# Attention's softmax denominators inverted on one row per head and spread by DMA, and 13 more exponential pairs on VectorE

## The chip, the cores and the metric

One Trainium2 chip, one core. The metric is the device time of one execution in microseconds (us), lower is better. Each kernel is timed as the median of several runs. In the profile PE is TensorE, PEld its weight loads, DVE is VectorE, ACT is ScalarE, POOL is GpSimd and SP is SyncE, whose queue issues nearly all DMAs.

## The reference

The input is x, 2048 tokens by 1024, bfloat16. Four residual layers run one after the other: A, B, A, B, with the same weights in both rounds.

```
x = x + A(layernorm(x)); x = x + B(layernorm(x)); x = x + A(layernorm(x)); x = x + B(layernorm(x))

A:  32 heads of 32; phi(q) = concat(softmax(q w_phi), softmax(-q w_phi)), the same for k
    o = phi(q) (phi(k)^T v) / (phi(q) sum(phi(k)) + 1e-6);  return o @ wo
B:  32 heads of 32; scores = q k^T * 32**-0.5
    o = softmax(scores) v;  return o @ wo
```

A is linear attention and B is plain, non-causal softmax attention over all 2048 keys. The change is in B.

## The kernel before

Nothing is issued in the order in which the source reads. Every piece of work is registered as an `Op` with an engine, an estimated duration, dependencies, the buffers that it needs and a due time (`prio`). `Sched.run` (L145) is a list scheduler: it plays the operations on modelled engines, takes the earliest due one whose buffers can be had, and so fixes one order per engine, which is the order of the program. SBUF is one arena out of which buffers are taken by class; `QUOTA` (L257) says how many of a class may live at once. PSUM's eight banks are given out in the same way: two groups of three banks for scores (class S), bank 6 for the accumulator (class acc), bank 7 for everything that fills in between (`FIL`). Where PE would idle too long, the scheduler puts filler matmuls in (L1248, L1253).

`attention` (L971) is called once per round, after layer A and the first keys, values and queries. It runs over 32 turns; a turn is one chunk of 512 queries (qc, four of them) with one group of four heads (g, eight of them). `turns` (L1100) lists them: first chunks 0 and 1 for every group, then chunks 2 and 3. `pos` is a turn's number, 0 to 31. Every turn has two halves (pp), each with two heads' outputs: 16 key blocks, written as d (8) and pairs, with four units per step of d. A unit is 128 keys by 512 queries of one head.

Three units are one group: three score matmuls (L1006) into three banks, one ACTIVATE with Exp over 1536 columns (L1012, ACT), then per unit two matmuls into the accumulator (L1042): one with v, one with a matrix of ones, so that the 128 partitions of bank 6 hold the numerators of two heads in 64 rows and their denominators, each repeated on 32 rows, in the other 64. At the end of each half DVE copies the bank into a buffer of class T (L1057), which frees it for the next half.

Some units do not go to ACT. `exp_dve` (L931) takes two units of head 3 of the group and computes the exponential by a polynomial on DVE: a score matmul into bank 7 (L944), two DVE steps that read it (L949, L952), twice, then two steps on exponents (L955, L958), three on the polynomial (L963) and the product (L966). `EXTRA` (L270) lists, for each round and turn, which pairs (pp, d) go that way; `LEAD` makes them due half a turn early.

At the end of a turn the denominators are inverted (L1083 to L1095). In the halves of one turn they lie on opposite partitions, so two DMAs of 64 rows each bring them from the two T buffers into one buffer (class den) of 128 partitions by 512; four DVE reciprocals of 128 columns (L1087) invert it, and two DVE products (L1091) write the turn's 128 by 512 bfloat16 output tile (class oT). The last turn of a round (`end`) has a way of its own, without DMA (L1064 to L1082).

Meanwhile the other work of the layer fills in: keys and values of later groups (L839 on DVE, copies L831 into kT), queries (L847, L863, L852 and L853; chunks 2 and 3 are stored to DRAM by L865 and come back by L871 to L873), weights (L522), the output projection (L899, or L928 at the end), and in the first round also the next layer A's norms and keys.

Of the kernel before, what the change touches and what calls it, by code (L numbers as in the profile page):

```python
# [11 lines left out]
ALU = mybir.AluOpType  # L12
AX = mybir.AxisListType
BF16 = mybir.dt.bfloat16
F32 = mybir.dt.float32
# [5 lines left out]
C512 = 512  # L21
# [26 lines left out]
class Sched:  # L48
# [11 lines left out]
    def op(self, eng, dur, fn, deps=(), bufs=(), prio=0.0, lat=None, mode=None):  # L60
        o = Op(eng, dur, LAT[eng] if lat is None else lat, fn, tuple(bufs), prio, mode, len(self.ops))
        for d in deps:
            if d is not None:
                d.out.append(o)
                o.ndep += 1
        for b in o.bufs:
            b.left += 1
        self.ops.append(o)
        return o
# [75 lines left out]
    def run(self):  # L145
# [25 lines left out]
        while left:  # L171
# [85 lines left out]
QUOTA = {"pk": 3, "pv": 2, "kv": 1, "ln": 2, "mm": 2, "cmp": 2, "bc": 4, "num": 1, "wt": 4, "fil": 2,  # L257
         "e": 6, "vp": 6, "e1": 4, "vp1": 4, "E": 5, "q2": 3, "kt": 3, "w2": 8, "w2o": 3, "oT": 26, "T": 4, "den": 2,
         "lnt": 6, "lnw": 2, "lnw1": 1, "eq": 8, "ns": 4, "cw": 6, "hl": 6, "oc": 2, "slab": 7, "slabk": 3, "fin": 4,
         "rs": 8, "pkf": 1, "part": 8, "w2r": 1,  # L260
         "xs": 1, "xu": 2, "xg": 2, "xx": 2, "E1": 3}
SPELL = 3.4
KEEP = 0.75
# [3 lines left out]
POW2_0 = 0.998010015430466  # L267
POW2_C = (-2.753493604392706, 3.611980637904819, -2.738565741928622)
LEAD = 5.0
EXTRA = (lambda i: [(i % 2, 2)] if 12 <= i < 17 else [],  # L270
         lambda i: [(0, 2), (1, 2)] if 16 < i < 30 and i % 4 else [(i % 2, 2)] if 8 <= i < 30 else [])


def act_us(n):
# [3 lines left out]
def dve_us(n):  # L278
    return n / 960 + 0.15
# [6 lines left out]
def kernel(  # L286
# [11 lines left out]
    nc = tc.nc  # L298
    P = nc.NUM_PARTITIONS
    _, S, D = A_x.shape  # L300
    PO = D // P
    G = PO
    NC = S // C512
# [14 lines left out]
    dram_p = ctx.enter_context(tc.tile_pool(name="scratch", bufs=1, space=bass.MemoryType.DRAM))  # L318
# [23 lines left out]
    for j in range(4):  # L342
# [4 lines left out]
        out=rep[:].rearrange("p (x j) -> p x j", j=4),  # L347
        in_=J_bf[:].rearrange("p (j d) -> p d j", d=32)[:, 0:8, :],
    )
    nc.vector.tensor_copy(out=fold[:], in_=ident[:, 0:32])  # L350
    for a in range(1, 4):
        nc.vector.tensor_tensor(
            out=fold[:], in0=fold[:], in1=ident[:, 32 * a:32 * a + 32], op=ALU.add
# [4 lines left out]
        out=selb[:].rearrange("p (j d) -> p j d", d=32),  # L358
        in_=pick[:].unsqueeze(2).to_broadcast([P, 4, 32]),
# [10 lines left out]
    wdq_v = wd_q[:].rearrange("(po pi) f -> pi po f", pi=P)  # L370
    wdk_v = wd_k[:].rearrange("(po pi) f -> pi po f", pi=P)

    qd = dram_p.tile([P, 2 * G * C512], BF16, tag="qd")
    qd_v = qd[:].rearrange("p (c g n) -> p c g n", c=2, g=G)
    xd = dram_p.tile([P, 3 * PO * C512], BF16, tag="xd")
# [3 lines left out]
    op = sch.op  # L379

    def sb(cls, *dims, dt=BF16):
        n = 1
        for d in dims:
            n *= d
        b = Buf("sb", -(-n * (4 if dt == F32 else 2) // 64) * 64, cls)
        b.with_ = ()

        def v():
            ap = arena[:, b.at // 2:b.at // 2 + n * (2 if dt == F32 else 1)]
            if dt == F32:  # L390
                ap = ap.bitcast(F32)
            if len(dims) == 2:
                ap = ap.rearrange("p (a b) -> p a b", a=dims[0])
            elif len(dims) == 3:
                ap = ap.rearrange("p (a b c) -> p a b c", a=dims[0], b=dims[1])
            return ap

        return b, v
# [16 lines left out]
    def dma(prio, fn, deps=(), bufs=(), q="SP", kb=256, issue=0.55):  # L415
        return op(q, issue, fn, deps, bufs, prio, lat=2.0 + kb / 200.0)
# [450 lines left out]
    def q_back(g, c, prio, away):  # L867
        q_b, q_v = sb("q2", 2, C512)
        src = qd_v[:, c - 2, g, :]
        return q_b, q_v, [  # L870
            dma(prio, lambda: nc.sync.dma_start(out=q_v()[:, 0, :], in_=src), [away], [q_b], kb=128),  # L871
            dma(prio, lambda: nc.sync.dma_start(out=q_v()[64:128, 1, :], in_=src[0:64]), [away], [q_b], kb=64),
            dma(prio, lambda: nc.sync.dma_start(out=q_v()[0:64, 1, :], in_=src[64:128]), [away], [q_b], kb=64)]  # L873
# [97 lines left out]
    def attention(base, kT, vT, q_of, gate, extra):  # L971
# [14 lines left out]
        n = 0  # L986
        i = 0
        while i < len(units):
# [5 lines left out]
            qc, g, pp, d, j = grp[0]  # L994
            prio = base + 10 * pos[(qc, g)] + 5 * pp + 0.5 * d
# [7 lines left out]
            def sfn(grp=grp, s_v=s_v):  # L1003
# [9 lines left out]
                out=e_v()[:, 0:w * C512], in_=s_v(), func=ACT.Exp, scale=4 * math.log(2)),  # L1013
# [7 lines left out]
        if True:  # L1021
            for qc, g in turns:
                T = []
                end = (qc, g) == turns[-1]
                for pp in range(2):
                    a_b, a_v = ps("acc", [(6,)])
                    last = None
                    for d in range(8):
                        prio = base + 10 * pos[(qc, g)] + 5 * pp + 0.5 * d
# [30 lines left out]
                prio = base + 10 * pos[(qc, g)] + 12  # L1060
                lo_, hi_ = slice(0, 64), slice(64, 128)
                d_b, d_v = sb("den", C512, dt=F32)
                r_b, r_v = d_b, d_v
                if end:  # L1064

                    o_b, o_v = sb("oT", C512)
                    rc = [op("DVE", 128 * 8 / 960 + 0.12, lambda b=b, T=T, r_v=r_v: nc.vector.reciprocal(
                        out=r_v()[hi_, b * P:(b + 1) * P], in_=T[0][1]()[hi_, b * P:(b + 1) * P]),
                        [T[0][2]], [d_b, T[0][0]], prio) for b in range(4)]
                    s = [op("DVE", dve_us(512), lambda o_v=o_v, r_v=r_v, T=T: nc.vector.tensor_tensor(  # L1070
                        out=o_v()[lo_, :], in0=T[0][1]()[lo_, :], in1=r_v()[hi_, :], op=ALU.mult),
                        rc, [o_b, d_b, T[0][0]], prio)]
                    l_b, l_v = sb("den", C512, dt=F32)
                    ln = op("ACT", act_us(512), lambda l_v=l_v, a_v=a_v: nc.scalar.activation(
                        out=l_v()[lo_, :], in_=a_v()[lo_, :], func=ACT.Ln), [last], [a_b, l_b], prio)
                    ln = op("ACT", act_us(512), lambda l_v=l_v: nc.scalar.activation(
                        out=l_v()[lo_, :], in_=l_v()[lo_, :], func=ACT.Exp, scale=-1.0), [ln], [l_b], prio)
                    s.append(op("DVE", dve_us(512), lambda o_v=o_v, l_v=l_v, a_v=a_v: nc.vector.tensor_tensor(
                        out=o_v()[hi_, :], in0=a_v()[hi_, :], in1=l_v()[lo_, :], op=ALU.mult),
                        [ln], [o_b, l_b, a_b], prio))  # L1080
                    oTs[qc][g] = (o_b, o_v, s)
                    continue  # L1082
                m1 = dma(prio, lambda d_v=d_v, T=T: nc.sync.dma_start(out=d_v()[hi_, :], in_=T[0][1]()[hi_, :]),  # L1083
                         [T[0][2]], [d_b, T[0][0]], kb=128)
                m2 = dma(prio, lambda d_v=d_v, T=T: nc.sync.dma_start(out=d_v()[lo_, :], in_=T[1][1]()[lo_, :]),
                         [T[1][2]], [d_b, T[1][0]], kb=128)
                rc = [op("DVE", 128 * 8 / 960 + 0.12, lambda b=b, d_v=d_v, r_v=r_v: nc.vector.reciprocal(  # L1087
                    out=r_v()[:, b * P:(b + 1) * P], in_=d_v()[:, b * P:(b + 1) * P]), [m1, m2], [d_b], prio)
                    for b in range(4)]
                o_b, o_v = sb("oT", C512)  # L1090
                s = [op("DVE", dve_us(512), lambda a=a, b=b, k=k, o_v=o_v, r_v=r_v, T=T: nc.vector.tensor_tensor(  # L1091
                    out=o_v()[a, :], in0=T[k][1]()[a, :], in1=r_v()[b, :], op=ALU.mult),
                    rc, [o_b, r_b, T[k][0]], prio)
                    for k, (a, b) in enumerate(((lo_, hi_), (hi_, lo_)))]
                oTs[qc][g] = (o_b, o_v, s)  # L1095
        return oTs, so

# [9 lines left out]
        out=phi()[32 * j:32 * j + 32, :, 32 * j:32 * j + 32],  # L1107
        in_=A_w_phi.rearrange("(g j) i f -> j i g f", j=4)[j]), [phi_0], [phi_b], kb=16) for j in range(4)]
# [14 lines left out]
    for layer in range(2):  # L1123
# [21 lines left out]
        else:  # L1145
            wq_s = [slab("slab", second - 15 + fc, wdq_v[:, :, fc * C512:(fc + 1) * C512], C512, [store["q"][fc]])
                    for fc in range(2)]
            for c in range(NC - 1):
                x_b, x_v = sb("xn", PO, C512)
                xnA[c] = (x_b, x_v, [dma(second - 20 + 20 * c, lambda c=c, x_v=x_v: nc.sync.dma_start(  # L1150
                    out=x_v(), in_=xd_v[:, c, :, :]), [xnA[c]], [x_b], kb=1024)] * 4)
# [11 lines left out]
        for c in range(NC):  # L1163
            pr = second + 20 * c
            o_b, o_v = sb("oc", G, C512)
# [21 lines left out]
        for g in range(G):  # L1187
            pr = at + 10 * pos[(0, g)]
            w = slab("w2", pr - 11, B_w[:, :, g * P:(g + 1) * P], P) if g else wq0
            for qc in range(NC):  # L1190
# [3 lines left out]
                else:  # L1194
                    away = q_away(g, qc, pr + 2 + 6 * (qc - 2), w, FIL)
                    q_of[(qc, g)] = q_back(g, qc, at + 10 * pos[(qc, g)] - 12, away)
        oTs, last_s = attention(at, kT, vT, q_of, gate, EXTRA[layer])
        if last:
            bo_s = [slab("slab", at + 160 + fc, B_o[:, :, fc * C512:(fc + 1) * C512], C512) for fc in range(2)]
# [14 lines left out]
        qc = NC - 1  # L1214
# [9 lines left out]
        if not last:  # L1224
            r_b, r_v = sb("w2r", 2, D)
# [11 lines left out]
        if not last:  # L1237

            kv = new_kv()
            for c, p0 in ((0, 190), (1, 220), (2, 265)):  # L1240
# [4 lines left out]
                    out=xd_v[:, c, :, :], in_=xv()), fin, [xb], kb=1024)  # L1245
# [43 lines left out]
```

## Time and profile before

| | us |
|---|---|
| median of 3 runs | 2510.38 (2509.66 to 2510.57) |
| the profiled execution | 2511.27 |
| its span, first to last instruction | 2509.5 |
| attention of round one, first to last L1012 or L1057 | about 358 to 1346 |
| attention of round two | about 1566 to 2499 |
| granted TensorE clock, mean | 0.994 |

The profiled execution is 0.9 us above the median, and 1.8 us of it lie outside its span. A turn takes about 30 us. Busy shares are given per engine over the span and in 40 slices of it; the waits name the engine that came last.

### The profile page before, as it was taken

What the parts mean: (1) busy time and instruction counts of PE and PEld (TensorE: products, weight loads), DVE (VectorE), ACT (ScalarE), POOL (GpSimd) and SP (SyncE); (2) the same over time, 40 slices, a digit from 0 to 9 for tenths busy, and PEclk for the clock granted to TensorE, in tenths of its full rate; (3) what the DMA queues carried; (4) which work ended last, traced back from release to release, by engine and by line L of the source; (5) the groups of instructions that cost most, each with busy time, mean ns of one, the idle gap of its engine ahead of it and who ended that gap; (6) DMA issues with size and microseconds to landing.
All of it is one profiled execution on the core that took longest, in us unless ns stands there. A gap on an engine that the chain in (4) does not pass through costs nothing.

```text
span 2509.5 us, 62924 instructions
## 1 busy us (share of the span) xinstructions
PE 2368.6 (94%) x27872; PEld 893.4 (36%) x27872; DVE 1468.5 (59%) x2003; ACT 2145.4 (85%) x1897; POOL 26.1 (1%) x72
## 2 busy tenths in 40 slices
PE   7999999999999999999999999999999999999998
PEld 4443433333333333333333444333333333333333
DVE  6997653333356345654646766333356578687854
ACT  6335558999999999999996465699999999999998
POOL 0000000000000000000000000000000000000000
PEclk9999999999999999999999999999999999999999
DMA  9110012111121222222323001111121100110000
GB/s 219 33 44 1 22 21 48 35 36 44 41 62 42 56 54 69 77 66 69 114 65 116 1 5 38 36 36 35 40 62 27 35 27 27 29 33 27 25 25 27
DMA packets 185282, 117.39 MB, mean 47 GB/s; under 512 B 103344, under 2 KB 175024, under 8 KB 184240
## 3 DMA queue, kind: packets, MB, share of 16 engines
q1 hardware_dynamic: 183952, 111.26, 16.7%
q8 instruction: 218, 3.57, 0.6%
q10 hardware_dynamic: 1056, 2.10, 0.3%
q14 instruction: 56, 0.46, 0.1%
HBM read 62.46 MB, written 15.73 MB: 31 GB/s over the span
## 4 chain that ended last, share of the span: by engine, by line
ACT 46%; PE 31%; issue 12%; DVE 8%; SPq 1%; DMA 1%; ACTq 0%; DVEq 0%
ACT arena L1012 43%; PE psum L421 14%; PE psum L425 5%; PE psum L1042 5%; PE psum L1006 4%; DVE arena L616 1%; SPq L456 1%; PE psum L1253 1%; PE psum L780 1%; ACT arena L612 1%; DVE arena L625 1%; DVE arena L963 1%; DVE arena L662 1%; DVE arena L510 1%; DVE arena L514 1%
## 5 line engine op out<-in xcount | busy, mean ns | idle before, releaser
L1012 ACT ACTIVATE arena<-psum 128x1536 bf16<-128x1536 f32 x1342 | 1812.4, 1566 | 50.5 <-PE psum L1006 43.7
L1042 PE MATMUL psum<-arena 128*32 128x512 bf16 x4096 | 699.0, 385 | 11.6 <-ACT arena L1012 8.4
L1042 PE MATMUL psum<-arena,ones_bf 128*32 128x512 bf16 x4096 | 700.3, 386 | 0.0
L1006 PE MATMUL psum<-arena 32*128 32x512 bf16 x4022 | 522.8, 383 | 74.6 <-ACT arena L1012 68.3
L425 PE MATMUL psum<-arena 128*32 128x512 bf16 x8256 | 576.3, 380 | 4.9 <-DVE arena L625 1.3
L421 PE MATMUL psum<-arena 128*128 128x512 bf16 x2032 | 474.2, 383 | 18.1 <-DVE arena L514 5.4
L1006 PEld LDWEIGHTS <-arena 32*128 32x128 bf16 x4022 | 163.4, 91 | 574.8 <-issue 564.9
L421 PEld LDWEIGHTS <-arena 128*128 128x128 bf16 x2032 | 193.6, 98 | 265.8 <-issue 47.6
L425 PEld LDWEIGHTS <-arena 128*32 128x32 bf16 x8256 | 212.3, 96 | 209.8 <-issue 53.9
L1042 PEld LDWEIGHTS <-arena 128*32 128x32 bf16 x4096 | 165.8, 94 | 271.6 <-issue 246.5
L1087 DVE RECIPROCAL arena<-arena 128x128 f32<-128x128 f32 x248 | 212.9, 913 | 44.7 <-DMA arena<-arena 44.4
L1253 PE MATMUL psum<-xT,zero 128*32 128x512 bf16 x2712 | 218.5, 382 | 0.0
L839 DVE CAST arena<-psum 128x512 bf16<-128x512 f32 x112 | 77.3, 690 | 238.5 <-PE psum L425 238.1
L1042 PEld LDWEIGHTS <-ones_bf 128*32 128x32 bf16 x4096 | 158.4, 94 | 62.7 <-issue 50.8
L1057 DVE COPY arena<-psum 128x512 f32<-128x512 f32 x126 | 86.8, 689 | 157.3 <-PE psum L1042 155.6
L963 DVE SCALAR_TENSOR_TENSOR arena<-arena 128x1024 f32<-128x1024 f32 x111 | 135.6, 1222 | 2.3
L612 ACT ACTIVATE arena<-psum 128x512 bf16<-128x512 f32 x80 | 42.8, 600 | 86.1 <-PE psum L421 57.8
L742 ACT ACTIVATE arena<-psum 128x512 bf16<-128x512 f32 x128 | 69.8, 597 | 41.5 <-PE psum L421 32.0
L625 DVE TENSOR_TENSOR arena<-psum,arena 128x1024 bf16<-128x1024 f32 x64 | 78.3, 1224 | 39.6 <-PE psum L425 35.5
L510 DVE TENSOR_TENSOR arena<-xT,arena 128x1024 f32<-128x1024 bf16 x64 | 77.9, 1219 | 35.2 <-ACT arena L499 34.8
L1253 PEld LDWEIGHTS <-zero 128*32 128x32 bf16 x2712 | 70.3, 97 | 64.5 <-issue 16.8
L514 DVE TENSOR_TENSOR arena<-arena 128x1024 bf16<-128x1024 f32 x64 | 77.4, 1223 | 23.9 <-ACT arena L504 22.6
(100 smaller groups left out, 1428.3 us busy)
## 6 DMA issues: line engine op xcount, KB each, us to landing
arena<-arena SPq DMA_DIRECT2D x124, 128.0 KB, 2.2
arena<-in_A_wqkv_dram SPq DMA_DIRECT2D x10, 1024.0 KB, 5.5
arena<-in_B_wqkv_dram SPq DMA_DIRECT2D x32, 256.0 KB, 3.1
arena<-arena SPq DMA_DIRECT2D x256, 32.0 KB, 1.9
arena<-in_B_wo_dram SPq DMA_DIRECT2D x32, 256.0 KB, 3.0
arena<-wd_k SPq DMA_DIRECT2D x8, 1024.0 KB, 5.7
arena<-in_A_wo_dram SPq DMA_DIRECT2D x4, 1024.0 KB, 7.1
arena<-in_B_wqkv_dram SPq DMA_DIRECT2D x4, 1024.0 KB, 5.4
```

Of the source, the lines that this page charges most:

```text
L421: nc.tensor.matmul(out_, lhsT=lhsT, rhs=rhs, start=start, stop=stop, skip_group_check=True)
L425: nc.tensor.matmul(out_[ks, :], lhsT=lhsT[:, ks], rhs=rhs, start=start, stop=stop, tile_position=(0, 32 * k), skip_group_check=True)
L510: s1 = op("DVE", dve_us(1024), lambda pr=pr, w_v=w_v: nc.vector.tensor_tensor(out=w_v(), in0=xT[:, pr, csl(c)], in1=m_v().unsqueeze(1).to_ ...
L514: fin.append(op("DVE", dve_us(1024), lambda pr=pr, w_v=w_v: nc.vector.tensor_tensor(out=xv()[:, pr, :], in0=w_v(), in1=r_v().unsqueeze(1). ...
L625: ml = op("DVE", dve_us(1024), lambda vpv=vpv, wv_=wv_, sv=sv: nc.vector.tensor_tensor(out=wv_()[:, :, :, 0:DH], in0=vpv().rearrange("p (h ...
L963: last = [op("DVE", dve_us(1024), lambda i=i, c=c: nc.vector.scalar_tensor_tensor(out=x_v(), in0=(x_v() if i else g_v()), scalar=c, in1=g_ ...
L1006: nc.tensor.matmul(out=s_v()[:, x * C512:(x + 1) * C512], lhsT=kT[g][1]()[r, pp, d * P:(d + 1) * P], rhs=q_of[(qc, g)][1]()[r, (pp + j // ...
L1012: ex = op("ACT", act_us(w * C512), lambda s_v=s_v, e_v=e_v, w=w: nc.scalar.activation(out=e_v()[:, 0:w * C512], in_=s_v(), func=ACT.Exp, s ...
L1042: nc.tensor.matmul(out=a_v()[col:col + 32, :], lhsT=v_v()[:, kc % 4, o:o + DH] if what == 0 else ones_bf[:], rhs=ev()[:, x * C512:(x + 1) ...
L1057: cp = op("DVE", dve_us(512), lambda t_v=t_v, a_v=a_v: nc.vector.tensor_copy(out=t_v(), in_=a_v()), [last], [a_b, t_b], prio - 4)
L1087: rc = [op("DVE", 128 * 8 / 960 + 0.12, lambda b=b, d_v=d_v, r_v=r_v: nc.vector.reciprocal(out=r_v()[:, b * P:(b + 1) * P], in_=d_v()[:, b ...
L1253: nc.tensor.matmul(psum[32 * k:32 * k + 32, 6 * C512:7 * C512], lhsT=zero[:], rhs=xT[:, 0, 0:C512], start=False, stop=False, tile_position ...
```

## The change

The inversion of the denominators is done on one row per head instead of 32 equal ones, and `exp_dve` takes more units. The `end` turn is as it was.

- From each T buffer a DMA takes one row of each of the two heads (512 numbers) and lays it over 32 partitions by 16 columns; the two DMAs fill a buffer of 128 by 16 (class cden).
- One DVE reciprocal of 16 columns inverts all four heads' rows.
- A DMA writes the 128 by 16 numbers to a DRAM scratch `rd`, where they are four rows of 512; another reads each row back onto 32 partitions, into the den buffer.
- The two products read it on the same partitions as the numerators.
- `EXTRA` lists 10 pairs instead of 5 in the first round and 40 instead of 32 in the second.

```diff
-         "rs": 8, "pkf": 1, "part": 8, "w2r": 1,
+         "rs": 8, "pkf": 1, "cden": 2, "part": 8, "w2r": 1,
...
-EXTRA = (lambda i: [(i % 2, 2)] if 12 <= i < 17 else [],
-         lambda i: [(0, 2), (1, 2)] if 16 < i < 30 and i % 4 else [(i % 2, 2)] if 8 <= i < 30 else [])
+EXTRA = (lambda i: [(0, 2), (1, 2)] if 12 <= i < 17 else [],
+         lambda i: ([(0, 2), (1, 2)] if i % 3 else [(0, 2), (0, 5), (1, 4)]) if 16 <= i < 30 else [(i % 2, 2)] if 8 <= i < 16 else [])
...
+    rd = dram_p.tile([2 * NC * G * 4, C512], F32, tag="rd")
+    rd_v = rd[:].rearrange("(t h) n -> t h n", h=4)
+    gone = []
...
-                m1 = dma(prio, lambda d_v=d_v, T=T: nc.sync.dma_start(out=d_v()[hi_, :], in_=T[0][1]()[hi_, :]),
-                         [T[0][2]], [d_b, T[0][0]], kb=128)
-                m2 = dma(prio, lambda d_v=d_v, T=T: nc.sync.dma_start(out=d_v()[lo_, :], in_=T[1][1]()[lo_, :]),
-                         [T[1][2]], [d_b, T[1][0]], kb=128)
-                rc = [op("DVE", 128 * 8 / 960 + 0.12, lambda b=b, d_v=d_v, r_v=r_v: nc.vector.reciprocal(
-                    out=r_v()[:, b * P:(b + 1) * P], in_=d_v()[:, b * P:(b + 1) * P]), [m1, m2], [d_b], prio)
-                    for b in range(4)]
+                c_b, c_v = sb("cden", 16, dt=F32)
+                at_d = rd_v[len(gone)]
+                gone.append((qc, g))
+                m = [dma(prio, lambda k=k, c_v=c_v, T=T: nc.sync.dma_start(
+                    out=c_v()[64 * k:64 * k + 64, :],
+                    in_=T[k][1]()[64 * (1 - k):64 * (1 - k) + 64:32, :].rearrange("r (s c) -> r s c", c=16)),
+                    [T[k][2]], [c_b, T[k][0]], kb=4) for k in range(2)]
+                rc = op("DVE", 0.27, lambda c_v=c_v: nc.vector.reciprocal(out=c_v(), in_=c_v()), m, [c_b], prio)
+                aw = dma(prio, lambda c_v=c_v, at_d=at_d: nc.sync.dma_start(
+                    out=at_d.rearrange("h (s c) -> (h s) c", c=16), in_=c_v()), [rc], [c_b], kb=8)
+                bk = dma(prio, lambda r_v=r_v, at_d=at_d: nc.sync.dma_start(
+                    out=r_v(), in_=at_d.unsqueeze(1).to_broadcast([4, 32, C512])), [aw], [d_b], kb=256)
                 o_b, o_v = sb("oT", C512)
-                s = [op("DVE", dve_us(512), lambda a=a, b=b, k=k, o_v=o_v, r_v=r_v, T=T: nc.vector.tensor_tensor(
-                    out=o_v()[a, :], in0=T[k][1]()[a, :], in1=r_v()[b, :], op=ALU.mult),
-                    rc, [o_b, r_b, T[k][0]], prio)
-                    for k, (a, b) in enumerate(((lo_, hi_), (hi_, lo_)))]
+                s = [op("DVE", dve_us(512), lambda a=a, k=k, o_v=o_v, r_v=r_v, T=T: nc.vector.tensor_tensor(
+                    out=o_v()[a, :], in0=T[k][1]()[a, :], in1=r_v()[a, :], op=ALU.mult),
+                    [bk], [o_b, r_b, T[k][0]], prio)
+                    for k, a in enumerate((lo_, hi_))]
```

In the changed kernel's numbering the new DMAs are L1090 (twice a turn), L1095 (the write) and L1097 (the read), the reciprocal is L1094 and the product L1100; lines between the two places of the diff stand 3 higher than before (L1012 becomes L1015), lines behind it 9 higher.

## The prediction

> **What bounds the kernel now.** I read the busy lines of the page first, then its chain, then the windows and the waits inside one stretch of attention. Columns of the groups: line, engine, operation, tiles and shapes, count | busy us, mean ns | idle us before it.
>
> ```profile
> PE 2368.6 (94%) x27872; PEld 893.4 (36%) x27872; DVE 1468.5 (59%) x2003; ACT 2145.4 (85%) x1897; POOL 26.1 (1%) x72
> ...
> DVE  6997653333356345654646766333356578687854
> ACT  6335558999999999999996465699999999999998
> ...
> ACT 46%; PE 31%; issue 12%; DVE 8%; SPq 1%; DMA 1%; ACTq 0%; DVEq 0%
> ...
> L1012 ACT ACTIVATE arena<-psum 128x1536 bf16<-128x1536 f32 x1342 | 1812.4, 1566 | 50.5 <-PE psum L1006 43.7
> ...
> L1087 DVE RECIPROCAL arena<-arena 128x128 f32<-128x128 f32 x248 | 212.9, 913 | 44.7 <-DMA arena<-arena 44.4
> ...
> L963 DVE SCALAR_TENSOR_TENSOR arena<-arena 128x1024 f32<-128x1024 f32 x111 | 135.6, 1222 | 2.3
> ```
>
> ACT is full in two blocks of slices (8 to 21 and 27 to 39, of 62.7 us each): the attentions of the two layers. PE is full as well, but its matmuls are pipelined and part of them are fillers, so busy shares do not decide it. The waits do. First the window 2000 to 2400 us (busy us and counts of PE, PEld, DVE, ACT, POOL, then clock, DMA share, GB/s), then who waited for whom there (us in total, times, longest).
>
> ```profile
> 2000.00:2400.00 400.00, 371.61 (x5112) 128.14 (x5109) 317.94 (x386) 398.62 (x298) 0.00 (x0) 1.00 0.11 29
> ```
>
> ```profile
> PE psum L1006 <- ACT arena L1012: 22.2, 68, 1.0
> ...
> PE psum L1042 <- DVE arena L1057: 1.2, 4, 0.5
> PE psum L944 <- DVE arena L952: 0.4, 1, 0.4
> ```
>
> PE waits for ACT 68 times, for DVE 5 times. ACT's own waits there come to 1.3 us. So ACT's exponentials set the pace, and DVE, at 79% busy in its most loaded stretch, does not. One L1012 goes by every 400 / 298 = 1.342 us (its 1.566 us overlap) and holds three units of 512 columns: a unit costs 0.447 us of the path. The granted clock is 1.00.
>
> **Exponentials taken from ACT.** Each `exp_dve` call takes two units. Layer 0 goes from 5 calls to 10 (turns 12 to 16), layer 1 from 32 to 40: turns 8 to 15 keep one each, 16 to 29 go from 24 to 32. That is 13 calls, 26 units, and by the program's order the count of L1012 falls from 1342 to 1332. On the path: 26 x 0.447 = 11.6 us less. Each score moves from one form of matmul to another one by one, so PE's work stays; 61 fewer filler groups are issued, in places where PE would idle.
>
> **What they cost DVE.** By the rows, one call is 2 x (0.690 + 0.687) + 2 x 0.693 + 3 x 1.222 + 1.225 = 9.03 us; the timeline (start, length) shows dependent steps 0.73 apart instead of 0.69, so I use 9.2.
>
> ```profile
> 2314.86 0.69 DVE L949 TENSOR_SCALAR arena<-psum 128x512 f32<-128x512 f32 x1
> 2315.59 0.69 DVE L952 SCALAR_TENSOR_TENSOR arena<-arena,psum 128x512 f32<-128x512 f32 x1
> 2316.31 0.69 DVE L955 TENSOR_SCALAR arena<-arena 128x1024 f32<-128x1024 f32 x1
> ```
>
> 13 x 9.2 = 120 us more for DVE.
>
> **The reciprocals.** 248 of L1087 go, 212.9 us of DVE. In their place come 62 on 16 columns. Between 128x32 (L619, 353 ns) and 128x128 (913 ns) a column costs 5.8 ns, so 16 columns are 353 - 93 = 260 ns (ends: 166 ns, the 32x16 copy of L691, and 353): 16 us. DVE in total: -213 + 16 + 120 = -77 us. None of this is on the path by itself, since ACT is the pace; without the moved units it would be worth about nothing.
>
> **The DMAs.** Two of 128 KB per turn go; four come: two of 4 KB (L1090), one write of 8 KB to DRAM (L1095), one read of 256 KB spread over 32 partitions (L1097). Rows for them (KB each, median us to landing; the last line, from the instructions of L865, is of the qd writes):
>
> ```profile
> arena<-arena SPq DMA_DIRECT2D x124, 128.0 KB, 2.2
> ...
> arena<-in_B_wqkv_dram SPq DMA_DIRECT2D x32, 256.0 KB, 3.1
> arena<-arena SPq DMA_DIRECT2D x256, 32.0 KB, 1.9
> ...
> qd<-arena SPq DMA_DIRECT2D x32, 128.0 KB, 1.8
> ```
>
> ```profile
> DMA to landing us min/median/max: 1.7/1.8/7.9
> ```
>
> L1090: between 1.7 and 2.2, I take 1.9 (nearest, 512-byte runs). L1095: between 1.7 and 7.9; 1.8, the same direction. L1097: between 2.1 (128 KB from qd) and 3.1; 3.0, the same bytes. The way from the last PSUM copy to the finished tile was 2.2 + 3.4 + 1.4 = 7.0 us; it becomes 1.9 + 0.3 + 1.8 + 3.0 + 1.4, with some 0.4 of issue, 8.8 us. The tile is wanted turns later, except at the end, where turn 30 has its own 15 us before the last turn is done, and the last turn keeps its old way. So nothing on the path. The T buffers are held 2 us longer, of 13 us between two.
>
> The new waits stand in two queues. On DVE the product (L1100) waits for L1097, and behind it stand the next copy out of PSUM (L1060), which frees the only accumulator, and the next exponential step, which frees bank 7; PE waits for both, and ACT for PE. What covers the 1.8 + 3.0 + 0.4 = 5.2 us is DVE's other work between reciprocal and product. By the program's order that is 5.8 to 8.4 us in 14 of the 15 loaded turns of layer 1 (2.1 us in turn 19). In the light turns it is mostly under 3 us, but there DVE idles anyway: busy 87.5 of 240 us from 450 to 690, 65.8 of 190 from 1610 to 1800. On SP, L1095 waits for the reciprocal and L1097 for L1095's landing: 2 to 4 us per turn in which the copies to kT (L831), the q swaps, the stores and reloads of q and the weight loads stand behind. They are wanted up to a turn later; in the whole run ACT waited for a DMA once, 3.6 us. If that cover goes, a stop costs about that.
>
> **Is DVE still below the pace?** From the second half of turn 14 to the first half of 29 the new order has on DVE 33 calls (303.6 us), 30 copies and 22 casts at 0.69 (35.9), 28 products at 0.686 (19.2), 15 small reciprocals (3.9): 362.6 us. In 23 of the calls the second score of a call follows the first with nothing between, and waits for bank 7; L949 waited 54.3 us in 47 cases, 1.16 each: 26.7. Sum 389.3. ACT needs there 896 units x 0.447 = 400.5. So 11 us, 3%, are left; the same sum for the old order leaves 52. Half-turn by half-turn, DVE never falls over one L1012 behind. For the thinner margin I add one more stretch's ACT waits, 1.3 us.
>
> **The sum.** The profiled execution took 2511.27 us (span 2509.5), 0.9 above the median of 2510.38. 2511.3 - 11.6 + 1.3 = 2501.0, against the median 2500.1 us. A difference under 0.2%, 5 us, cannot be told from none.
>
> **Rivals.** (1) Slower: the write of 64-byte rows lands late and the products stop DVE. Every us over the cover counts in 15 turns, after the 11 us of room are used; it is a loss of over 5 us when the waits pass (11 + 11.6 + 5) / 15 = 1.8 us per turn, that is when L1095 needs over 1.8 + 1.3 + 1.8 = 4.9 us at a median cover of 6.5. At L865's worst, 7.9, the waits are 4.8 x 15 = 72, and the time 2500 + 72 - 11 = 2561. For it: the longest landing of the same kind, and that old L1087 waited 44.4 us for its DMA in 28 of 62 turns. Against: the median of 1.8, and only two of those waits, 3.2 us, lie in 1990 to 2430. [...] No run shown here has such a write to DRAM. 0.12.
>
> (2) No difference: SP stops. In turns 1 to 15 of both layers, three stops of the 3.65 us that L865 once caused take back 11 us: 2511. For it: two more waits per turn at the head of SP. Against: the one case in 2510 us. 0.10.
>
> (3) More than the sum: DVE's 197 freed us also shorten ACT's waits for PE. Without the first waits of both attentions (2 x 9.4) L1012's 43.7 are 25; a fifth of it makes 2495. 0.08.
>
> That the units do not leave ACT is excluded by the count of L1012.
>
> **How the numbers follow.** Forecast 0.70, at 2500.1; with (3) faster 0.78; same 0.10; slower 0.12. The range runs from (3)'s 2495 to 2508, two of (2)'s stops over the forecast; what lies outside is most of (1) and part of (2).
>
> **What would show it.** Right: L1015 (L1012 before) 1332 times at the same step, PE waiting for ACT and not for DVE in the loaded turns, L1094 near 0.26 us, L1095 landing near 2 us, L1100's waits for a DMA under 11 us in the loaded turns. Wrong: PE waiting for L1060 or L955 (L952 before) by tens of us, or ACT waiting for PE in turns 16 to 29 of layer 1.

## The result: slower by 14%

| | us |
|---|---|
| changed kernel, median of 4 runs | 2868.74 (2867.26 to 2875.41) |
| kernel before on the same chip, median of 4 runs | 2510.02 (2509.13 to 2510.57) |
| ratio, 95% interval | 1.1435 (1.1415 to 1.1455) |
| the profiled execution after, and its span | 2875.41, 2873.6 |
| attention of round one, and of round two, before, from the first exponential to the start of the last turn's last product | 988.0, 932.9 |
| the same after | 1190.7, 1091.8 |

The forecast was 2500.1. Both attentions lost: 203 and 159 us, which is the whole difference of the two spans (364.1 us) within 3 us.

### The profile after

The page's busy lines, three of its 40-slice lines, the start of the chain and the costliest group (columns as before):

```profile
PE 2481.2 (86%) x27562; PEld 895.6 (31%) x27628; DVE 1383.7 (48%) x1947; ACT 2161.7 (75%) x1887; POOL 26.2 (1%) x72
...
DVE  6986632111446324443324765221344476668653
ACT  5345568878877888888787465788878888888887
...
PEclk9999999999988999999889999999999998999989
...
ACT 3%; PE 2%; issue 1%; DMA 1%; DVE 0%; ACTq 0%; SPq 0%
...
L1015 ACT ACTIVATE arena<-psum 128x1536 bf16<-128x1536 f32 x1332 | 1826.8, 1468 | 387.3 <-DMA arena<-arena 245.0
```

ACT had nines in both attentions before; now it has sevens and eights. It did not get more to do: the exponentials take 1826.8 us against 1812.4, for 1332 instructions instead of 1342. Its idle time ahead of them went from 50.5 to 387.3 us, 337 of the 364. Two thirds of that idle time is put down to a DMA from the arena into the arena, which no such wait of ACT had before. DVE is less busy than it was. The chain covers 7% of the span and breaks off, so it does not help here.

The waits of the whole run (us, times, longest):

```profile
ACT arena L1015 <- DMA arena<-arena: 245.0, 112, 9.8
...
PE psum L1009 <- ACT arena L1015: 224.8, 231, 6.4
...
DVE arena L1100 <- DMA arena<-rd: 105.7, 37, 9.7
...
ACT arena L1015 <- PE psum L1009: 80.7, 85, 9.4
```

The source view of L1090, the gather of the denominators, names the DMA (who waited for it: us, times), and SP's own waits say what held that DMA:

```profile
L1090 SPq DMA_DIRECT2D arena<-arena x124: 507/554/619, 403.3 to 2832.5; - x124
...
ACT arena L1015: 245.0, 112
DVE arena L842: 67.5, 18
DVE arena L1094: 58.2, 30
POOL arena L633: 56.6, 4
```

```profile
SPq L1090 <- DVE arena L1060: 418.9, 81, 17.6
...
SPq L1090 <- ACT arena L1015: 83.4, 76, 3.9
```

112 of the 124 DMAs stopped ACT. Nothing that ACT reads or writes is in the buffer of 128 by 16 that L1090 fills; only the reciprocal L1094 needs it. DVE's casts of keys and values (L842) do not need it either, and they waited 67.5 us for it. The other way round, the DMA has to wait for the copy L1060, which fills the T buffer, but it also waited for exponentials. The timeline shows one case (start, length, engine, line; in brackets the idle time before and who ended it):

```profile
703.69 4.14 ACT L1015 ACTIVATE arena<-psum 128x1536 bf16<-128x1536 f32 x3
...
707.86 0.55 SPq L1090 DMA_DIRECT2D arena<-arena  x1
...
709.70 0.25 DVE L1094 RECIPROCAL arena<-arena 128x16 f32<-128x16 f32 x1 [2.25 <-DMA arena<-arena]
709.74 2.40 SPq L834 DMA_DIRECT2D arena<-arena  x4
709.78 6.82 ACT L1015 ACTIVATE arena<-psum 128x1536 bf16<-128x1536 f32 x5 [1.95 <-DMA arena<-arena]
```

ACT's exponential ends at 707.83. L1090 is issued 0.03 us later: it waited for that exponential. It lands 1.84 us after its issue, and in the same tenth of a us the reciprocal and the next exponential start. So the DMA stands between two ACT instructions as if it touched what both of them write.

The windows view of 2000 to 2400 us, the stretch from which the pace was taken:

```profile
2000.00:2400.00 400.00, 332.65 (x4254) 109.01 (x4252) 189.70 (x248) 332.67 (x245) 0.00 (x0) 0.94 0.11 31
```

245 exponentials instead of 298 pass in 400 us, DVE is busy 190 us instead of 318, and the granted clock is 0.94 instead of 1.00.

### The profile page after: what moved, and what is told of

The parts are those of the page before. It is cut to its first block, busy times and chain, and to the rows that moved or that the text cites. A ratio compares the mean times of both kernels' runs of the same rounds, so it can differ in the third digit from the quotient of the medians.

```text
span 2873.6 us, 62681 instructions
## 1 busy us (share of the span) xinstructions
PE 2481.2 (86%) x27562; PEld 895.6 (31%) x27628; DVE 1383.7 (48%) x1947; ACT 2161.7 (75%) x1887; POOL 26.2 (1%) x72
## 5 line engine op out<-in xcount | busy, mean ns | idle before, releaser
L1015 ACT ACTIVATE arena<-psum 128x1536 bf16<-128x1536 f32 x1332 | 1826.8, 1468 | 387.3 <-DMA arena<-arena 245.0
L1045 PE MATMUL psum<-arena 128*32 128x512 bf16 x4096 | 737.1, 409 | 16.8 <-DVE arena L1060 9.3
L1009 PE MATMUL psum<-arena 32*128 32x512 bf16 x3996 | 548.1, 405 | 230.6 <-ACT arena L1015 224.8
L1045 PE MATMUL psum<-arena,ones_bf 128*32 128x512 bf16 x4096 | 738.3, 409 | 0.0
L428 PE MATMUL psum<-arena 128*32 128x512 bf16 x8256 | 619.3, 404 | 84.6 <-DVE arena L842 40.1
L424 PE MATMUL psum<-arena 128*128 128x512 bf16 x1973 | 467.4, 383 | 24.6 <-DVE arena L517 5.4
L428 PEld LDWEIGHTS <-arena 128*32 128x32 bf16 x8256 | 219.9, 100 | 325.6 <-issue 179.3
L1045 PEld LDWEIGHTS <-arena 128*32 128x32 bf16 x4096 | 165.4, 95 | 297.8 <-issue 273.4
L842 DVE CAST arena<-psum 128x512 bf16<-128x512 f32 x112 | 77.4, 691 | 349.1 <-PE psum L428 275.2
L1262 PE MATMUL psum<-xT,zero 128*32 128x512 bf16 x2664 | 232.4, 407 | 0.0
L966 DVE SCALAR_TENSOR_TENSOR arena<-arena 128x1024 f32<-128x1024 f32 x150 | 183.2, 1221 | 14.1 <-PE psum L1045 11.1
L1100 DVE TENSOR_TENSOR arena<-arena 64x512 bf16<-64x512 f32 x124 | 84.9, 685 | 117.5 <-DMA arena<-rd 105.7
L1060 DVE COPY arena<-psum 128x512 f32<-128x512 f32 x126 | 86.6, 687 | 99.0 <-PE psum L1045 96.1
L952 DVE TENSOR_SCALAR arena<-psum 128x512 f32<-128x512 f32 x100 | 68.9, 689 | 112.0 <-PE psum L947 92.1
L628 DVE TENSOR_TENSOR arena<-psum,arena 128x1024 bf16<-128x1024 f32 x64 | 78.4, 1225 | 73.3 <-PE psum L428 55.5
```

Of the source, the lines that this page charges most:

```text
L424: nc.tensor.matmul(out_, lhsT=lhsT, rhs=rhs, start=start, stop=stop, skip_group_check=True)
L428: nc.tensor.matmul(out_[ks, :], lhsT=lhsT[:, ks], rhs=rhs, start=start, stop=stop, tile_position=(0, 32 * k), skip_group_check=True)
L628: ml = op("DVE", dve_us(1024), lambda vpv=vpv, wv_=wv_, sv=sv: nc.vector.tensor_tensor(out=wv_()[:, :, :, 0:DH], in0=vpv().rearrange("p (h ...
L842: return op("DVE", dve_us(512), lambda: nc.vector.tensor_copy(out=dst(), in_=src()), [dep], bufs, prio)
L966: last = [op("DVE", dve_us(1024), lambda i=i, c=c: nc.vector.scalar_tensor_tensor(out=x_v(), in0=(x_v() if i else g_v()), scalar=c, in1=g_ ...
L1009: nc.tensor.matmul(out=s_v()[:, x * C512:(x + 1) * C512], lhsT=kT[g][1]()[r, pp, d * P:(d + 1) * P], rhs=q_of[(qc, g)][1]()[r, (pp + j // ...
```

## The experiments

**Theory A:** the form of L1090's source is the cause. It takes two rows 32 partitions apart out of T (`[a:a+64:32, :]`), and with this access waits stand between the DMA and exponentials that share no data with it: ACT waited for 112 of the 124 (245.0 us), and the DMA for an exponential in 76 cases (83.4 us). That the access is booked as touching far more of the arena than its two rows is the author's guess at the reason; no run here shows how the program comes by these waits. The order of waits in the program has them as well: counted from the place where the DMA is registered, how many ACT instructions later does the first one stand that waits for it?

| kernel and DMA | first ACT instruction that waits |
|---|---|
| changed kernel, L1090, two rows | the very next one for 118 of 124 (at most 2 later); it is L1015 for 120 |
| the same with one-row DMAs | 8 later at the least |
| before, L1083 (64 rows without a step) | 14 later at the least |
| before, L1085 | 5 later at the least |

In the same order 120 of the 124 two-row DMAs themselves wait for an ACT instruction, and 7 of the 248 one-row ones.

**Rivals:** the chain through DRAM (L1095, L1097) and the products that wait for it in DVE's queue, or SP's queue, or DVE's new load. Each run is compared with the kernel before on the same chip. "One-row DMAs", "The two rows alone" and both runs of "The inversion alone, and the units alone" share one chip (kernel before: median 2508.66). The old units with the 16-row kernel and the last run share a third (2509.51). All others share a second (2508.49).

### One-row DMAs

```diff
-    in_=T[k][1]()[64 * (1 - k):64 * (1 - k) + 64:32, :]...) for k in range(2)]
+    in_=T[k][1]()[64 * (1 - k) + 32 * h:64 * (1 - k) + 32 * h + 1, :]...) for k in range(2) for h in range(2)]
```

Each of the two DMAs becomes two of one row (four per turn), into the matching 32 partitions; nothing else changes.

> The changed kernel, but each of the two DMAs that take two rows 32 partitions apart out of a T buffer (L1090) is split into two DMAs of one row each: four per turn, same bytes, same result. Theory A (the two-row access is booked as touching far more of the arena than it does, so it waits for ACT's last write and ACT's next write waits for it): in the program's order the first ACT instruction that waits for such a DMA stands 8 or more behind it instead of 0, the 245 us of ACT waiting for arena<-arena are gone, and the time falls from 2869 to the forecast's neighbourhood, 2495 to 2515 us. Rival B (the 64-byte DRAM write lands late and the products stop DVE): the DRAM way is unchanged, the time stays above 2800. Rival C (13 more exponential pairs overload DVE): stays above 2800.

Measured: 2536.51 us, ratio 1.0106 (1.0090 to 1.0122). 332 of the 359 us are gone, though the time is still 21 us over the range that theory A gave. ACT's and DVE's groups, from the lines view (idle time before, with all its releasers):

```profile
L1015 ACT ACTIVATE arena<-psum 128x1536 bf16<-128x1536 f32 x1332 | 1804.6, 1549 | 84.5 <-PE psum L1009 64.8 <-PE psum L1045 8.2 <-DVE arena L1100 4.1
```

```profile
L1100 DVE TENSOR_TENSOR arena<-arena 64x512 bf16<-64x512 f32 x124 | 84.9, 685 | 153.7 <-DMA arena<-rd 145.5 <-DMA arena<-arena 4.1 <-PE psum L1045 2.1
```

Who waited for the gather now (source view of L1090):

```profile
DVE arena L1094: 43.0, 25
POOL arena L633: 14.6, 2
```

ACT no longer waits for the gather, though twice as many DMAs are issued. What is left is 28 us over the kernel before, and a second cause: the products wait 145.5 us for the read L1097. It lies in round one (attention 1015.2 against 988.0 before; round two 932.0 against 932.9).

### The two rows alone, read by nobody

To the kernel before only the two-row gather of every turn is added, into a buffer that nothing uses (its class cden is added to `QUOTA`, as in the change):

```diff
+                c_b, c_v = sb("cden", 16, dt=F32)
+                for k in range(2):
+                    dma(prio, lambda k=k, c_v=c_v, T=T: nc.sync.dma_start(
+                        out=c_v()[64 * k:64 * k + 64, :],
+                        in_=T[k][1]()[64 * (1 - k):64 * (1 - k) + 64:32, :].rearrange("r (s c) -> r s c", c=16)),
+                        [T[k][2]], [c_b, T[k][0]], kb=4)
```

> The kernel before, and beside its own way two DMAs per turn that take the two rows 32 partitions apart out of the T buffers into a small buffer that nobody reads; denominators inverted as before, EXTRA as before, nothing goes through DRAM. Theory A: 124 such DMAs at about 3 us each of stopped ACT: 2800 to 2900 us. Rivals B and C: 2510 to 2515, four small DMAs more on a queue with room.

Measured: 2865.11 us, ratio 1.1420 (1.1404 to 1.1437). From its lines view:

```profile
L1012 ACT ACTIVATE arena<-psum 128x1536 bf16<-128x1536 f32 x1342 | 1836.7, 1476 | 371.4 <-DMA arena<-arena 255.9 <-PE psum L1006 80.6 <-PE psum L1042 28.8
```

The whole loss comes from 124 DMAs of 4 KB whose data nobody reads. No reciprocal, no DRAM, no product and no moved unit is needed for it. 356 us over 124 is 2.9 us each. A wait itself is 255.9 / 112 = 2.3 us; most of the rest stands as waits for PE (80.6 and 28.8 against 43.7 and 1.2 before). PE for its part waits for the exponentials to give it a bank back, 248.8 us before L1006 against 68.3.

### The same with one-row DMAs, read by nobody

As above with four one-row DMAs per turn.

> The companion of the two-row kernel: the kernel before, and beside its own way four DMAs of one row each per turn into the small buffer that nobody reads. Theory A (it is the two-row access, not the small DMAs): within 10 us of 2509, as the ACT queue waits for none of them soon; if small DMAs or SP's issue time are what costs, it stays hundreds of us above.

Measured: 2502.50 us, ratio 0.9976 (0.9967 to 0.9985). The same group on this run's page:

```profile
L1012 ACT ACTIVATE arena<-psum 128x1536 bf16<-128x1536 f32 x1342 | 1810.7, 1582 | 42.3 <-PE psum L1006 41.1
```

Number, queue and bytes of the DMAs are thus not the cause; twice as many in the one-row form cost nothing. Nor is any work saved here, and yet it is 6 us faster than the kernel before, probably because a few DMAs more make the list scheduler place other things otherwise. Differences of this size between two orders say nothing of an edit.

Two other differences between the pair are ruled out by kernels of this document. The two-row DMA fills 64 partitions instead of 32, but so do L1083 and L1085 of the kernel before, and they stop ACT nowhere (all its waits for DMAs in that trace are 4.9 us for the first loads of x and 3.6 us for `qd`). It takes more than one row, but the 16-row kernel below takes four adjacent rows in each DMA, and ACT is not stopped by them either (5.2 us of waits for DMAs, all for x). What is left is the step over partitions.

### The inversion alone, and the units alone

The changed kernel with the old `EXTRA`, and the kernel before with the new one:

> The changed kernel with the EXTRA lists of before: only the new way of inverting the denominators. Theory A: all of the loss is here, 2510 + 360 to 370, so 2850 to 2890 us. Rival B: the same, 2850 to 2890. Rival C: about 2510.

Measured: 2891.18 us, ratio 1.1522 (1.1506 to 1.1538), one us over the expected range. ACT's wait for the gather:

```profile
ACT arena L1015 <- DMA arena<-arena: 262.3, 113, 10.0
```

The inversion holds the loss; the moved units, if anything, lessened it.

> The kernel before with only the new EXTRA lists (26 more units by DVE); denominators inverted as before. Theory A: not slower by hundreds; either 2499 (gain of 11.6 us kept) or, since the four long reciprocals stay and DVE has 13 x 9.2 = 120 us more, up to some 30 us worse in the loaded turns: 2495 to 2540. Rival B: the same, nothing goes through DRAM here. Rival C: above 2700.

Measured: 2525.90 us, ratio 1.0069 (1.0056 to 1.0082). The window 2000 to 2400 of this run, and ACT's waits in the whole run:

```profile
2000.00:2400.00 400.00, 369.47 (x5135) 131.10 (x5131) 354.23 (x426) 378.20 (x281) 0.00 (x0) 1.00 0.10 27
```

```profile
ACT arena L1012 <- PE psum L1006: 50.6, 41, 9.4
...
ACT arena L1012 <- PE psum L1042: 11.8, 8, 3.7
```

With 60 long reciprocals still in the loaded turns ACT is busy 378 of 400 us and the attention of round two takes 949.0, 16 more than before. By the prediction's sum for those turns that is 389.3 - 3.9 + 60 x 0.913 = 440 us on DVE against ACT's 400.5, 40 too many. The run is 17 us over the kernel before, or 29 over that kernel less the 11.6 us that the units were to bring, so the sum has the direction right and the size too high. DVE is close to full: from 1990 to 2430 it is busy 390.1 us and waits another 28.0 for the scores of its own calls, 418 of 440. The two parts of the change need each other.

### The read booked longer

What remains in the one-row kernel? The scheduler books the read with 2.0 + 256/200 = 3.3 us, and puts the products in DVE's order by that. The DMA's records say more: its 128 packets of 2 KB run from 1.37 to 4.67 us after the issue (medians), and the product starts at least 4.8 us after it. So the products may stand in DVE's queue too early, and behind them the copies that free banks 6 and 7. The edit tells the planner only (kb=640 instead of 256, that is 5.2 us):

```diff
-   out=r_v(), in_=at_d.unsqueeze(1).to_broadcast([4, 32, C512])), [aw], [d_b], kb=256)
+   out=r_v(), in_=at_d.unsqueeze(1).to_broadcast([4, 32, C512])), [aw], [d_b], kb=640)
```

> The one-row kernel (2536.5 us) with one number changed: the planner books 5.2 us instead of 3.3 us for the read that spreads the reciprocals (kb=640 for 256), so that it places the products later in DVE's order. The read took 4.9 us from issue to the product's start there, and DVE stood still 145 us for it in 47 cases. Theory D (what is left of the loss is DVE standing at products that come too early in its queue, with the copies that free banks 6 and 7 behind them): DVE's wait for arena<-rd falls under 70 us and the time to 2500 to 2522. Theory E (SP's queue and the four small DMAs are what is left): no change, 2530 to 2540.

Measured: 2496.33 us, ratio 0.9953 (0.9940 to 0.9965). The read is as long as it was (1.37 to 4.68), but the waits are:

```profile
DVE arena L1100 <- DMA arena<-rd: 55.5, 22, 8.1
```

That is 145.5 to 55.5, and 38 to 40 us of time (by the two ratios, or as measured on two chips) from a number in the planner. It is a little under the expected range.

### The read from 16 rows

The gather brings four of the 32 equal rows of each head, laid over 32 partitions by 64 columns; the scratch has 16 rows, and each is spread to 8 partitions instead of four rows to 32. The bytes that the read writes into SBUF are the same. The run asks whether the read's 3.3 us hang on the number of rows in its source. (The sizes of the scratch, of the gather, of the write and of the reciprocal follow; only the main lines are shown.)

```diff
-   c_b, c_v = sb("cden", 16, dt=F32)
+   c_b, c_v = sb("cden", 64, dt=F32)
...
-   out=r_v(), in_=at_d.unsqueeze(1).to_broadcast([4, 32, C512])), [aw], [d_b], kb=256)
+   out=r_v(), in_=at_d.unsqueeze(1).to_broadcast([16, 8, C512])), [aw], [d_b], kb=256)
```

> The one-row kernel, but the small buffer holds 128 by 64 numbers, every denominator four times, so that the DRAM scratch holds 16 rows of 512 and the read spreads each onto 8 partitions instead of 4 rows onto 32; the reciprocal has 64 columns, some 0.54 us instead of 0.26. [...]

Measured: 2494.55 us, ratio 0.9945 (0.9932 to 0.9957), 13.9 us faster than the kernel before on that chip. The 128 packets now run from 1.36 to 2.61 us after the issue: 1.25 us instead of 3.3. Up to 19 of them are under way at a time, against 6 with four rows (medians of 62). A packet is not quicker than before: 84 ns in both kernels (median), 94 ns on average with four rows and 101 with 16. More of them run at once: 128 packets of 94 ns in 3.3 us are 3.6 at a time on average, 128 of 101 ns in 1.25 us are 10.3. Why more run at once with 16 rows is not shown; the records here do not name the engine of a packet. The run's page, its window and its waits:

```profile
PE 2346.4 (94%) x27458; PEld 884.3 (35%) x27524; DVE 1400.5 (56%) x1947; ACT 2132.5 (86%) x1887; POOL 25.5 (1%) x72
...
ACT  6335548999999999999997455699999999999998
```

```profile
2000.00:2400.00 400.00, 371.69 (x5030) 127.07 (x5028) 341.90 (x417) 398.91 (x298) 0.00 (x0) 1.00 0.10 31
```

```profile
PE psum L1009 <- ACT arena L1015: 68.8, 211, 1.4
...
DVE arena L1100 <- DMA arena<-rd: 59.3, 28, 5.4
...
ACT arena L1015 <- PE psum L1009: 43.8, 35, 9.4
```

This is the profile that the prediction described: nines back on ACT, PE waiting for ACT, ACT waiting as little as before, DVE below it with 342 of 400 us. Attentions: 983.3 and 920.2. Its gathers of four rows are waited for by DVE's reciprocal (43.6 us in 28 cases) and once by POOL, never by ACT in this trace.

### Old units with the one-row and with the 16-row kernel

Both have the old `EXTRA`; each prices the 26 units against its partner.

> The one-row kernel with the EXTRA lists of before: the new inversion alone, without the two-row access. If the 26 units are worth their 11.6 us or more once DVE is relieved: 2545 to 2560 us, that is slower than the 2536.5 of the one-row kernel by 9 to 24. If DVE is the bound in the loaded turns and the 26 units are worth nothing: 2530 to 2537.

Measured: 2543.01 us, ratio 1.0139 (1.0124 to 1.0155). Against 2536.51 the units are worth 6.5 us with the slow read in DVE's queue, or 8 by the two ratios, since the two ran on different chips. It lies between the two expected ranges.

> The inversion with one-row DMAs and the read from 16 rows, but with the units of exponentials of the kernel before (5 and 32 pairs). It tells the price of the 26 units where the inversion itself stalls nothing. By the prediction's term of 0.447 us per unit it is 11.6 us slower than the same kernel with the new units (2494.6), so 2506, within 6 us of the kernel before. If the gain of that kernel comes from the cheaper inversion and not from the units, it stays near 2495. If the new order's waits of DVE eat part of the units' worth, it lies between, near 2500.

Measured: 2506.85 us, ratio 0.9989 (0.9980 to 0.9998). Against 2494.55 the units are worth 12.3 us, or by the two ratios 0.0044 x 2510 = 11.0, since these two ran on different chips as well. The inversion without them gains 2.7, less than a new order alone can move.

### The 16-row read booked longer

`kb=512` instead of 256 in the 16-row kernel.

> One-row DMAs, the read from 16 rows, and the new units, with the read booked 1.3 us longer in the order's planning (4.6 instead of 3.3 us). If products that stand too early in DVE's queue still cost something, their waits for the read (59.3 us in 28 cases in the kernel without this) fall by half and the time goes to about 2490. If these waits lie in places where DVE idles anyway, the time stays at 2494.6 within the 6 us that a new order alone moves it.

Measured: 2499.19 us, ratio 0.9960 (0.9946 to 0.9974). The waits for the read fall:

```profile
DVE arena L1100 <- DMA arena<-rd: 22.2, 8, 5.7
```

The time does not follow; it is 4.6 us longer, inside what a new order alone moves. So the waits that the 16-row kernel still has cost no more than a new order does.

## Why the prediction was wrong

**"So nothing on the path", and "The new waits stand in two queues".** This is the step that failed, and with it the sign. There were three queues: ACT's is the third. The prediction costed L1090 by its landing time alone, 1.9 us, and asked only who reads what it writes. It did not ask which instructions the program makes wait for a DMA with that access. Every gather cost 2.9 us on the path, 124 of them (the run with the two rows alone). Neither a rival nor a sign of being wrong named a wait of ACT for the gather. The prediction used the order of the changed program for what lies on DVE only; for ACT the same order holds the answer, the very next instruction waits.

**The landing times.** L1090 at 1.9 was right (1.84 in the case shown). L1095 at 1.8 was a little high for most turns: L1097, which waits for it, is issued as early as 1.4 us after L1095, and the write's 128 packets of 64 bytes end 1.04 us after the issue (median). L1097 at 3.0, with 3.1 as the upper bound, was wrong: 4.8 at the least. The bound came from a load of the same bytes whose source has many rows; the four-row source makes the difference, as the 16-row run shows (a product starts 3.1 us after the issue there, at the least).

**"In the light turns ... DVE idles anyway".** This was the second wrong step, worth some 40 us once the first is mended. It takes both a read that is longer than booked and a product that stands too early; the shorter read (2494.55 us) and the later product (2496.33) each take the loss away alone. In the one-row kernel the loaded turns did hold, as the cover worked out for them said: from 1990 to 2430 the products waited 10.7 us, under the 11 of room, and ACT's waits for PE and DVE came to 3.2. In round one, from 420 to 1300, it was otherwise:

```profile
DVE arena L1100 <- DMA arena<-rd: 84.0, 25, 8.1
...
ACT arena L1015 <- PE psum L1009: 27.8, 23, 4.8
...
PE psum L1045 <- DVE arena L1060: 7.6, 7, 2.6
```

and in the kernel before:

```profile
ACT arena L1012 <- PE psum L1006: 12.2, 15, 1.5
...
PE psum L1042 <- DVE arena L1057: 0.2, 1, 0.2
```

All waits of the exponentials in that stretch come to 40.7 us against 12.4, which is the 28 us that the one-row kernel loses. DVE's busy share is low in these turns, but each of its few copies frees a bank at a given time, and a product that stands ahead of it and waits makes it late.

**The pace, the units and the small costs were right.** 26 x 0.447 = 11.6 us was forecast for the units; 11.0 to 12.3 were measured once nothing stopped the queues. That so close a match came out is partly luck, as a new order alone moves the time by 6 us. L1015 counts 1332. The reciprocal of 16 columns was put at 0.26 us and takes 0.249; an `exp_dve` call goes by the rows used (its three polynomial steps took 1221 ns each on average, 1222 were used). DVE's total was to fall by 77 us and fell by 85:

```profile
L966 DVE SCALAR_TENSOR_TENSOR arena<-arena 128x1024 f32<-128x1024 f32 x150 | 183.2, 1221 | 14.1 <-PE psum L1045 11.1
...
L1094 DVE RECIPROCAL arena<-arena 128x16 f32<-128x16 f32 x62 | 15.5, 249 | 58.8 <-DMA arena<-arena 58.2
```

That the reciprocals are worth about nothing without the units was right as well (2.7 us). The sum of DVE's load was right in its direction: with the short reciprocals DVE stays below ACT, with the long ones it does not, though the run with the units alone lost less than the sum gives.

**The rivals.** (1) had the sign but not the mechanism. SP's waits for the write's landing in the changed kernel are these:

```profile
SPq L1097 <- DMA rd<-arena: 61.5, 45, 5.5
```

That is 1.4 us each on average, with a few late ones up to 5.5 us; but the kernel with the two rows alone loses as much without any write, and the 16-row kernel, which still has such waits (58.7 us in 44 cases), loses nothing. Its second half, products that stop DVE, did come, through the slow read and in the light turns. The write's 128 packets of 64 bytes were on their way for 0.2 us (median, first start to last end). (2), stops behind SP's new waits, did not come: in the 16-row kernel, which has both of them, ACT waits for a DMA only at the first loads of x (5.2 us in 2 cases; the kernel before has these too, 4.9 us in 2, beside the 3.6 us that the prediction counted as the only one). (3), more than the sum, has no run for it beyond the 6 us that any new order moves.

**What stays open.** Of the 332 us between the two-row and the one-row form ACT's idle time before its exponentials explains 387.3 - 84.5 = 303 and the exponentials' own longer time 22. How much of this is the lower granted clock was not tried apart from the stops. Why the program treats an access with a step over partitions in this way stays open too.

## What to carry to other kernels

Ask of every new DMA not only when it lands and who reads it, but which instructions the program makes wait for it. Here ACT, which sets the pace, stopped at 112 of 124 DMAs whose access had a step over partitions, at a cost of 2.9 us for each of the 124 (the two rows alone); with the same rows in pieces without a step it stopped at none of them, and the time was 2502.50 us instead of 2865.11. Where a planner orders the queues, look at its booked times too: the read was booked with 3.3 us, no product started earlier than 4.8 us after its issue, and that cost some 40 us over 62 transfers, because what stood behind the waiting instruction was late as well. DVE's low busy share in the light turns (in the kernel before 87.5 of 240 us from 450 to 690) did not cover the waits in its queue, by which the one-row kernel lost 28 us in round one: ask what the next instruction there frees, and for whom.

## What the hardware showed beyond what was expected

- The packets of a 256 KB read out of DRAM run for 3.3 us, first start to last end, with a source of 4 rows spread to 32 partitions each, and for 1.25 us with 16 rows spread to 8; a packet takes 84 ns in both (median).
- The mean granted clock was 0.938 to 0.943 in the profiled executions of the three kernels with the two-row gather, 0.991 in the two with the slow read booked too short, and 0.994 to 0.997 in the others. In these runs it is lower where PE stops more: PE's waits for other engines and for DMAs, added up from the waits view, are 362 to 384 us in the first three, 147 to 155 in the next two and 118 to 135 in the others. Whether it adds to the time by itself is not shown.
